# Attention and a mixture of experts on one core: the later attention lays the left block's scores over masked columns and turns each tile with three transposes

## The chip, the cores and the metric

One core of a Trainium2 chip runs the whole program in one launch. Its engines are TensorE (PE, with its weight loads PEld), VectorE (DVE), ScalarE (ACT), GpSimd (POOL) and SyncE (SP, which here only issues DMAs). The metric is the device time of one execution in microseconds (us); the median of three is compared.

## The reference, cut to what matters

```python
scores = q @ k.T / sqrt(D)                       # B,H,S,D = 4,8,768,64
rel = pos[:, None] - pos[None, :]
keep = (pos[None, :] < n_global) | ((rel >= 0) & (rel < n_local))    # 8 and 96
scores += -slope[h] * dist                       # dist = rel, or n_local for a far global key
a = softmax(where(keep, scores, -1e9)); x = a @ v
out = sum_e p[:, e] * (relu(x @ w1[e]) @ w2[e])  # 3072 rows, 512 -> 1024 -> 512, 4 experts
```

A row of queries sees at most 96 keys back, and the first 8 keys. So a tile of 128 queries needs its own block of 128 keys, the last 96 keys of the block on its left, and the global keys (32 columns are kept for them).

## The kernel before, in words

There are three stages. The first is the attention of batch 0 alone (0 to about 60 us). The second runs the experts of batches 0 and 1 and, woven into them, the attention of batches 1, 3 and 2 (`attention_chain`, about 100 to 646 us). The third is the experts of batches 2 and 3 (to the end). The change is in the second stage alone, the "later attention".

The later attention goes over 3 batches x 4 pairs of heads x 6 query tiles: 72 tiles, of which 12 are the first of their sequence (t = 0, with no left block) and 60 have one. It is a pipeline that moves by one `flow()` at a time, twelve flows to a pair. Each flow does, for four different tiles:

- `scores`: four fp32r matmuls (two heads, high and low parts) into one PSUM tile `ps`, per head 256 columns: 96 of the left block, 32 global, 128 of the own block. For t = 0 only the 128 of the own block are used.
- `softmax` of the tile whose scores are newest: per head one VectorE instruction that subtracts the bias `nbias`, writes `pb` and gives the row's extremum `nmax`, and one ScalarE exponential; then, of the tile before, the reciprocal of the row sums and one ScalarE multiplication per head (`pb <- pb, zsum`).
- `turn` of the tile before that: one PE transpose for each 128 columns of `pb` (four, or two at t = 0) into one PSUM bank `pt`, and one ScalarE copy to `pT`.
- `weigh`, once per pair of heads, when all six tiles are turned: per tile and head, `pT`'s own part times `v`, plus its left-and-global part times `vg`, into two `pt` banks.

`vg` holds, per tile, the 96 rows of `v` left of it and the 32 global rows. `windows` makes it with one SBUF-to-SBUF DMA on SP and one GpSimd copy, once per pair. Pools of this stage: `pb` 2 buffers, `pT` 6, `ps` 2, `pt` 2, `vg` 1, `v` 1.

In the same stage GpSimd makes sums and low parts of the experts' weights (`sums`, `w1s`, `w2s`, `raw`), fed by DMAs of raw weights; they are made for a unit two units ahead. An order is kept in program order only while `Ordered.on` is set or an engine is held; from step 14 of batch 0 on, where the attention's generator has run its first piece, a planner orders each engine's queue by priority and its own costs, and the queues then run in that order on the chip. How often a flow is emitted is paced by the matmul groups done (`paced`, `count`, `span`). All engines' calls go through the helper at L43, so nearly every row of the profile has that line; tiles tell them apart.

Of the kernel before, what the change touches and what calls it, by code (L numbers as in the profile page):

```python
# [186 lines left out]
def attn_moe_kernel(ctx: ExitStack, tc, q, k, v, n_global, n_local, domain_probs, w1, w2, out):  # L187
# [40 lines left out]

    nbias = fast.tile([P, H, 3 * P], BF16, name="nbias")

    def biases(sp):
# [152 lines left out]
    def windows(A, vt):  # L384
# [4 lines left out]
        return vg  # L389

    def scores(A, t, got):
# [13 lines left out]
        return [both[:, j] for j in range(2)]  # L405

# [13 lines left out]
    def softmax(A, new, old):  # L420
# [4 lines left out]
        if new:  # L425
            t, pr, ps = new["t"], new["pr"], new["ps"]
            cols = slice(0, P) if t == 0 else slice(0, 2 * P)
            bcol = slice(2 * P, 3 * P) if t == 0 else slice(0, 2 * P)
            new["pcol"] = pcol = slice(P, 2 * P) if t == 0 else slice(0, 2 * P)
            nmax = A.small.tile([P, 2], F32, name="nmax")  # L430
            new["zsum"] = A.small.tile([P, 2], F32, name="zsum")
            new["pb"] = A.pb.tile([P, 2, 2 * P], F32, name="pb")
        for j in range(2):
# [17 lines left out]
        if old:  # L451
            for j in range(2):
                p = pb[:, j, old["pcol"]]
                if A.early:
# [3 lines left out]
                else:  # L458
                    ac.activation(p, p, AF.Copy, scale=zsum[:, j : j + 1])

    def turn(A, tile_):
# [9 lines left out]
        tile_["pT"] = pT  # L471

    def weigh(A, three, x, b):

        px = A.px.tile([P, 512], F32, name=A.pxname)
        for i, tile_ in enumerate(three):
            t, pr, pT = tile_["t"], tile_["pr"], tile_["pT"]
            vt, vg = tile_["v"]["v"], tile_["v"]["vg"]
            for w in range(1 if t == 0 else 0, 2):
                for j in range(2):  # L480
                    vv = vt[:, j, t] if w == 1 else vg[:, j, t - 1]
                    te.matmul(
                        px[j * D : (j + 1) * D, i * P : (i + 1) * P],
                        vv,
                        pT[:, w, j, :],
                        start=(w == 1 if t == 0 else w == 0),
                        stop=(w == 1),
                    )
# [81 lines left out]
    def attention_chain(bs, A):  # L570
# [5 lines left out]
        def flow(new=None):  # L576

            one, two, three, four = tiles
            if new:
                new["ps"] = scores(A, new["t"], gots[new["m"]])  # L580
            if four:
# [6 lines left out]
            if three:  # L588
                turn(A, three)
            softmax(A, one, two)  # L590
# [7 lines left out]

        fetch_heads(0, "qkv")
        yield  # L600
        for m, (b, pr) in enumerate(order):
# [9 lines left out]
            for t in range(NQT):  # L611
                if t in (1, 2, 3):
                    if t == 1:
                        prepare_k(A, nat["k"], 1, got)
                    elif t == 2:
                        fetch_heads(m + 1, "qk")
                    else:
                        nat["vg"] = windows(A, nat["v"])
                    flow()
# [833 lines left out]
```

## Time and profile before

| | |
|---|---|
| median of three runs | 1162.91 us (1162.72 to 1163.08) |
| span of the profiled execution | 1162.9 us |
| PE / PEld busy | 1140.5 / 1062.6 us (98% / 91%) |
| DVE / ACT / POOL busy | 853.2 / 618.2 / 606.6 us (73% / 53% / 52%) |
| chain that ended last | PE 87%, DVE 5%, ACT 3%, POOL 2%, DMA 1% |

A matmul's record is longer than the time by which it moves the next one on, since matmuls are pipelined: the cost of a matmul is read as the distance from its start to the next start, not as its duration. An instruction's row names what it writes and reads (`pt<-ident,pb` is a transpose of `pb` into `pt`). The profiled execution and the median agree, so a sum made against the span holds for the median.

### The profile page before, as it was taken

The page shows a single profiled execution, that of the slowest core. Times are in us where ns is not written, and L with a number is a line of the kernel's source. Part 1 is how long each engine was busy: PE and PEld are TensorE (multiplying, and loading weights), DVE is VectorE, ACT ScalarE, POOL GpSimd, SP SyncE. Part 2 cuts the span into 40 slices and gives each one's busy share as a digit, 9 for nine tenths or more (in the row PEclk, how much of TensorE's full clock was granted, in tenths as well). Part 3 has the DMA queues.
Part 4 walks back from the last instruction along what each step waited for, and adds up shares of the span by engine and source line. Part 5 has one row for each costly group of instructions (what it writes and reads, how often), then busy time and mean ns, then how long its engine had stood idle before and what let it go on. Part 6 is the DMA issues. An engine that isn't in the chain of part 4 may idle for free.

```text
span 1162.9 us, 21146 instructions
## 1 busy us (share of the span) xinstructions
PE 1140.5 (98%) x7474; PEld 1062.6 (91%) x7474; DVE 853.2 (73%) x1944; ACT 618.2 (53%) x1597; POOL 606.6 (52%) x592
## 2 busy tenths in 40 slices
PE   7899999999999999999999999999999999999997
PEld 5678898989888989899998899999999999999997
DVE  7977776767767777776776777777777777777776
ACT  6854767777653665655565334444445444444443
POOL 5676645554343314222222327777778855555554
PEclk9999999999999999999999999999999999999999
DMA  9558798778775889978868668888887687777764
GB/s 185 149 172 290 268 294 258 269 253 255 247 261 206 282 269 286 282 234 279 257 196 288 207 215 304 306 302 300 284 314 281 240 303 239 249 247 247 245 232 131
DMA packets 181744, 294.32 MB, mean 253 GB/s; under 512 B 86400, under 2 KB 137088, under 8 KB 169344
## 3 DMA queue, kind: packets, MB, share of 16 engines
q1 hardware_dynamic: 177600, 286.61, 75.0%
q10 hardware_dynamic: 4032, 6.30, 1.5%
q8 instruction: 61, 1.00, 0.4%
q14 instruction: 51, 0.42, 0.1%
HBM read 207.93 MB, written 70.78 MB: 240 GB/s over the span
## 4 chain that ended last, share of the span: by engine, by line
PE 87%; DVE 5%; ACT 3%; POOL 2%; DMA 1%; issue 1%; DVEq 0%; ACTq 0%; POOLq 0%
PE pm L43 36%; PE pf L43 19%; PE X L43 11%; PE Y L43 9%; PE pt L43 7%; PE ps L43 4%; ACT pb L43 1%; DVE pb L43 1%; POOL w1s L43 1%; PE px L43 1%; DVE acc L43 1%; DVE xB L43 1%; DMA x_last<-piece 0%; DVE hA L43 0%; DVE pm L43 0%
## 5 line engine op out<-in xcount | busy, mean ns | idle before, releaser
L43 PE MATMUL pm<-w2s,h 128*128 128x512 f32 x1152 | 282.8, 395 | 3.6 <-DVE h L43 2.6
L43 PEld LDWEIGHTS pm<-w2s,h 128*128 128x128 f32 x1152 | 210.7, 188 | 46.5 <-DVE h L43 4.5
L43 ACT ACTIVATE hf<-pf 128x384 f32<-128x384 f32 x128 | 62.8, 491 | 248.3 <-DVE pf L43 247.1
L43 POOL TENSOR_TENSOR hS<-sf,hS 128x384 fp32r<-128x384 f32 x126 | 134.3, 1084 | 113.0 <-ACT hS L43 112.2
L43 DVE SCALAR_TENSOR_TENSOR acc<-pm,prob,acc 128x512 f32<-128x512 f32 x180 | 132.4, 748 | 54.5 <-PE pm L43 53.6
L43 POOL TENSOR_TENSOR sums<-raw 128x256 f32<-128x256 f32 x54 | 39.2, 745 | 211.8 <-DMA raw<-in_moe_w_dram 133.4
L43 PE MATMUL pm<-xT,w1s 128*128 128x384 f32 x744 | 147.9, 341 | 0.0
L43 PE MATMUL pf<-xT,w1s 128*128 128x384 f32 x768 | 146.5, 335 | 0.9 <-ACT hf L43 0.7
L43 PEld LDWEIGHTS pf<-xT,w1s 128*128 128x128 f32 x768 | 131.4, 188 | 1.7 <-ACT hf L43 1.2
L43 PEld LDWEIGHTS pm<-xT,w1s 128*128 128x128 f32 x744 | 128.0, 188 | 0.7 <-issue 0.7
L43 ACT ACTIVATE pb<-pb,nmax 128x256 f32<-128x256 f32 (+1 forms) x192 | 94.2, 498 | 58.1 <-DVE nmax L43 54.2
L43 DVE TENSOR_TENSOR hA<-hf,hA 128x384 fp32r<-128x384 f32 x94 | 84.6, 925 | 50.6 <-ACT hA L43 49.1
L43 PE MATMUL pm<-xB,w1s 128*128 128x384 f32 x574 | 116.8, 344 | 0.1
L43 PE MATMUL pf<-xB,w1s 128*128 128x384 f32 x576 | 110.7, 335 | 0.2 <-ACT hf L43 0.2
L43 PEld LDWEIGHTS pm<-xB,w1s 128*128 128x128 f32 x574 | 99.9, 188 | 5.5 <-issue 1.4
L43 ACT ACTIVATE h<-pm 128x384 fp32r<-128x384 f32 x128 | 62.0, 490 | 74.4 <-DVE pm L43 73.3
L43 PEld LDWEIGHTS pf<-xB,w1s 128*128 128x128 f32 x576 | 98.7, 188 | 0.6 <-ACT hf L43 0.4
L43 POOL TENSOR_TENSOR sf<-hf 128x384 f32<-128x384 f32 x63 | 70.3, 1116 | 43.6 <-ACT hf L43 43.6
L43 DVE CUSTOM_DVE_ANT_0 pb<-ps,nbias 128x256 f32<-128x256 f32 (+1 forms) x192 | 72.3, 395 | 5.8 <-PE ps L43 4.8
L43 DVE SCALAR_TENSOR_TENSOR h<-pm,h 128x384 fp32r<-128x384 f32 x128 | 69.5, 550 | 8.4 <-ACT h L43 6.8
L43 PE MATMUL Y<-w2b,hS 128*128 128x256 f32 x576 | 74.0, 282 | 0.0
L43 PE MATMUL X<-w2b,hS 128*128 128x256 f32 x576 | 73.9, 282 | 0.0
(159 smaller groups left out, 2183.5 us busy)
## 6 DMA issues: line engine op xcount, KB each, us to landing
w1s<-kept SPq DMA_DIRECT2D x47, 1792.0 KB, 8.2
w2b<-kept SPq DMA_DIRECT2D x224, 256.0 KB, 4.3
kept<-w1s SPq DMA_DIRECT2D x16, 1792.0 KB, 7.3
raw<-in_moe_w_dram SPq DMA_DIRECT2D x43, 512.0 KB, 4.7
kept<-w2s SPq DMA_DIRECT2D x16, 1024.0 KB, 6.9
w2s<-kept SPq DMA_DIRECT2D x16, 1024.0 KB, 5.5
qd<-qd SPq DMA_DIRECT2D x48, 192.0 KB, 3.2
v<-in_v_dram SPq DMA_DIRECT2D x16, 384.0 KB, 4.1
```

Source lines behind the costliest of these rows:

```text
L43: ins = fn(*args, **kwargs)
```

## The change

For tiles with a left block (t > 0) of the later attention:

- After the scores, a VectorE predicated copy lays the 96 left columns over columns 32 to 127 of the own block wherever that column's key lies after the query (mask `newer`, made once). The two never overlap: own key c is seen by query r if c <= r, the left key in column c if c > r.
- The bias is folded in the same way, once, by a minimum over `nbias`. Softmax then works on 160 columns (32 global, 128 folded) in place of 256.
- The normalised values go to a new tile `pn` of 320 columns by three ScalarE copies: own of head 0, global of head 0 (32 columns), global and own of head 1.
- `turn_folded` makes three transposes: own of head 0, own of head 1, and one that has both heads' globals in its first 64 columns. ScalarE copies own (256 columns) and, twice, 32 rows of globals. Two GpSimd affine selects (rows 32 to 63 and 64 to 127) copy the left part out of the folded block into `pT[:, 0]`, zero elsewhere.
- `pT[:, 1]` still has both parts, so `weigh` multiplies it by `v` of the own tile and `pT[:, 0]` by a difference: `differences` replaces `windows`, one GpSimd subtraction of neighbouring `v` tiles and one copy of the global rows; the DMA goes.

```diff
+    newer = fast.tile([P, NPREV], BF16, name="newer")
+    def differences(A, vt):
+        vd = A.vg.tile([P, 2, NQT - 1, D], F32, name="vg")
+        po.tensor_sub(vd, vt[:, :, : NQT - 1], vt[:, :, 1:])
+        po.tensor_copy(vd[:NGLOB], vt[:NGLOB, :, 0:1, :].to_broadcast([NGLOB, 2, NQT - 1, D]))
...
+            if t and not A.early:
+                own = new["both"][:, :, P + NGLOB :]
+                ve.copy_predicated(own, newer.bitcast(mybir.dt.uint16)[:, None, :].to_broadcast([P, 2, NPREV]), new["both"][:, :, :NPREV])
...
-            new["pb"] = A.pb.tile([P, 2, 2 * P], F32, name="pb")
+            new["pb"] = A.pb.tile([P, 2, width], F32, name="pb")
...
-                    ac.activation(p, p, AF.Copy, scale=zsum[:, j : j + 1])
+            old["pn"] = pn = A.pb.tile([P, 2 * PL], F32, name="pn")
+            glob = () if old["t"] == 0 else ((0, pn[:, P:PL], pb[:, 0, :NGLOB]),)
+            own = pn[:, PL:] if glob else pn[:, PL + NGLOB :]
+            for j, dst, src in ((0, pn[:, :P], pb[:, 0, NGLOB:]), *glob, (1, own, pb[:, 1, old["pcol"]])):
+                ac.activation(dst, src, AF.Copy, scale=zsum[:, j : j + 1])
+    def turn_folded(A, tile_):
+        t, pn = tile_["t"], tile_["pn"]
+        pt = A.pt.tile([P, 4, P], F32, name="pt")
+        pT = tile_["pT"] = A.pT.tile([P, 2, 2, P], F32, name="pT")
+        for place, at in enumerate((0, PL + NGLOB, P)[: 3 if t else 2]):
+            te.transpose(pt[:, place, :], pn[:, at : at + P], ident)
+        ac.copy(pT[:, 1], pt[:, :2])
+        if t:
+            for j in range(2):
+                ac.copy(pT[:NGLOB, 0, j], pt[j * NGLOB : (j + 1) * NGLOB, 2])
+            for rows in (slice(P // 4, P // 2), slice(P // 2, P)):
+                po.affine_select(
+                    pT[rows, 0], pT[rows, 1], pattern=[[0, 2], [-1, P]], compare_op=ALU.is_gt, fill=0.0,
+                    base=rows.start, channel_multiplier=1,
+                )
...
         fetch_heads(0, "qkv")
+        po.iota(
+            newer, pattern=[[1, NPREV]], base=NGLOB, channel_multiplier=-1, allow_small_or_imprecise_dtypes=True
+        )
+        po.tensor_scalar(newer, newer, 0.0, 1.0, op0=ALU.is_gt, op1=ALU.mult)
+        own = nbias[:, :, P + NGLOB : 2 * P]
+        ve.tensor_tensor(own, own, nbias[:, :, :NPREV], op=ALU.min)
...
-                        nat["vg"] = windows(A, nat["v"])
+                        nat["vg"] = differences(A, nat["v"])
```

## Rows read from the trace of the kernel before

**Rows 1.** The page: busy time by engine; PE's busy tenths in 40 slices

```profile
PE 1140.5 (98%) x7474; PEld 1062.6 (91%) x7474; DVE 853.2 (73%) x1944; ACT 618.2 (53%) x1597; POOL 606.6 (52%) x592
...
PE   7899999999999999999999999999999999999997
```

**Rows 2.** Busy us (instructions) by stretch, then granted clock, DMA share, GB/s

```profile
100.00:650.00 550.00, 546.37 (x3387) 495.68 (x3385) 401.04 (x950) 342.07 (x919) 210.80 (x207) 1.00 0.79 256
720.00:760.00 40.00, 40.00 (x287) 40.00 (x285) 30.04 (x52) 17.17 (x42) 32.33 (x32) 1.00 0.90 314
```

**Rows 3.** Groups of PE, 100:650: count | busy us, mean ns | idle before

```profile
L43 PE MATMUL pt<-ident,pb 128*128 128x128 f32 x264 | 41.3, 273 | 0.9 <-ACT pb L43 0.8
```

**Rows 4.** Timeline of PE, two turns: start us, merged length, count

```profile
145.31 0.49 PE L43 MATMUL pt<-ident,pb 128*128 128x128 f32 x3
145.55 0.60 PE L43 MATMUL pm<-xT,w1s 128*128 128x384 f32 x2
...
464.20 0.60 PE L43 MATMUL pt<-ident,pb 128*128 128x128 f32 x4
464.55 1.29 PE L43 MATMUL pm<-xT,w1s 128*128 128x384 f32 x6
```

**Rows 5.** Groups of DVE, 100:650, shapes apart

```profile
L43 DVE CUSTOM_DVE_ANT_0 pb<-ps,nbias 128x256 f32<-128x256 f32 x120 | 47.1, 418 | 4.0 <-PE ps L43 3.0
...
L43 DVE CUSTOM_DVE_ANT_0 pb<-ps,nbias 128x128 f32<-128x128 f32 x24 | 6.3, 281 | 0.0
```

**Rows 6.** Groups of ACT, 100:650, shapes apart

```profile
L43 ACT ACTIVATE pb<-pb,zsum 128x256 f32<-128x256 f32 x120 | 54.7, 503 | 10.3 <-DVE zsum L43 9.9
...
L43 ACT COPY pT<-pt 128x512 f32<-128x512 f32 x60 | 35.1, 585 | 8.7 <-PE pt L43 7.9
...
L43 ACT ACTIVATE pb<-pb,zsum 128x128 f32<-128x128 f32 x24 | 8.5, 396 | 1.9 <-DVE zsum L43 1.9
...
L43 ACT COPY pT<-pt 128x256 f32<-128x256 f32 x12 | 4.4, 364 | 0.2
```

**Rows 7.** Groups of POOL, whole span, shapes apart

```profile
L43 POOL TENSOR_TENSOR sums<-raw 128x256 f32<-128x256 f32 x54 | 39.2, 745 | 211.8 <-DMA raw<-in_moe_w_dram 133.4 <-DMA kept<-sums 54.2 <-DMA qd<-qd 24.0
...
L43 POOL COPY vg<-v 32x768 f32<-32x768 f32 x16 | 13.1, 821 | 33.6 <-DMA v<-in_v_dram 20.7 <-PE pm L43 12.2
...
L43 POOL TENSOR_TENSOR xB<-x,xB 128x768 fp32r<-128x768 f32 x6 | 11.0, 1845 | 0.0
...
masks.py:199 POOL TENSOR_SCALAR_AFFINE_SELECT ident<-ident 128x128 f32<-128x128 f32 x1 | 0.3, 292 | 0.1
```

**Rows 8.** Waits of PE, 100:650: total us, times, longest

```profile
PE pt L43 <- ACT pb L43: 0.8, 2, 0.4
```

**Rows 9.** DMA issues, 100:650: KB each, median us to landing

```profile
vg<-v SPq DMA_DIRECT2D x12, 288.0 KB, 6.5
```

**Rows 10.** Timeline of ACT: copies of a pair's last turned tile

```profile
146.03 0.59 ACT L43 COPY pT<-pt 128x512 f32<-128x512 f32 x1
...
397.52 0.59 ACT L43 COPY pT<-pt 128x512 f32<-128x512 f32 x1
...
479.56 0.59 ACT L43 COPY pT<-pt 128x512 f32<-128x512 f32 x1
```

**Rows 11.** Timeline of PE: `weigh` of a pair's last tile begins

```profile
149.62 0.39 PE L43 MATMUL pt<-pT,vg 128*64 128x128 f32 x4
...
402.40 0.39 PE L43 MATMUL pt<-pT,vg 128*64 128x128 f32 x4
...
483.48 0.39 PE L43 MATMUL pt<-pT,vg 128*64 128x128 f32 x4
```

**Rows 12.** Timeline of POOL near these: [idle before <- what ended it]

```profile
150.88 1.42 POOL L43 TENSOR_TENSOR sums<-raw 128x256 f32<-128x256 f32 x2 [7.67 <-DMA raw<-in_moe_w_dram]
...
153.08 0.74 POOL L43 TENSOR_TENSOR sums<-raw,sums 128x256 f32<-128x256 f32 x1
...
403.73 1.43 POOL L43 TENSOR_TENSOR sums<-raw 128x256 f32<-128x256 f32 x2 [12.42 <-DMA kept<-sums]
...
407.86 2.40 POOL L43 TENSOR_TENSOR sums<-sums,raw 128x1024 fp32r<-128x1024 f32 x1
...
480.98 2.38 POOL L43 TENSOR_TENSOR sums<-sums,raw 128x1024 fp32r<-128x1024 f32 x1
```

More of the change, by code (lines that the diff above doesn't have):

```diff
@@ L389, in windows @@
         return vg
+    def differences(A, vt):
+        vd = A.vg.tile([P, 2, NQT - 1, D], F32, name="vg")
+        po.tensor_sub(vd, vt[:, :, : NQT - 1], vt[:, :, 1:])
+        po.tensor_copy(vd[:NGLOB], vt[:NGLOB, :, 0:1, :].to_broadcast([NGLOB, 2, NQT - 1, D]))
+        return vd
     def scores(A, t, got):
@@ L404, in scores @@
                 )
-        return [both[:, j] for j in range(2)]
+        return both
     def scores_early(A, t0, got):
@@ L426, in softmax @@
             t, pr, ps = new["t"], new["pr"], new["ps"]
-            cols = slice(0, P) if t == 0 else slice(0, 2 * P)
-            bcol = slice(2 * P, 3 * P) if t == 0 else slice(0, 2 * P)
-            new["pcol"] = pcol = slice(P, 2 * P) if t == 0 else slice(0, 2 * P)
+            first = 0 if A.early else NPREV
+            cols = slice(0, P) if t == 0 else slice(first, 2 * P)
+            bcol = slice(2 * P, 3 * P) if t == 0 else slice(first, 2 * P)
+            width = 2 * P - first
+            new["pcol"] = pcol = slice(width - P, width) if t == 0 else slice(0, width)
+            if t and not A.early:
+                own = new["both"][:, :, P + NGLOB :]
+                ve.copy_predicated(own, newer.bitcast(mybir.dt.uint16)[:, None, :].to_broadcast([P, 2, NPREV]), new["both"][:, :, :NPREV])
             nmax = A.small.tile([P, 2], F32, name="nmax")
             new["zsum"] = A.small.tile([P, 2], F32, name="zsum")
-            new["pb"] = A.pb.tile([P, 2, 2 * P], F32, name="pb")
+            new["pb"] = A.pb.tile([P, 2, width], F32, name="pb")
         for j in range(2):
@@ L451, in softmax @@
         if old:
-            for j in range(2):
-                p = pb[:, j, old["pcol"]]
-                if A.early:
+            if A.early:
+                for j in range(2):
+                    p = pb[:, j, old["pcol"]]
                     ve.tensor_scalar(
@@ L457, in softmax @@
                     )
-                else:
-                    ac.activation(p, p, AF.Copy, scale=zsum[:, j : j + 1])
+                return
+            old["pn"] = pn = A.pb.tile([P, 2 * PL], F32, name="pn")
[3 more added lines that the diff above has]
+                ac.activation(dst, src, AF.Copy, scale=zsum[:, j : j + 1])
     def turn(A, tile_):
@@ L471, in turn @@
         tile_["pT"] = pT
+    def turn_folded(A, tile_):
[6 more added lines that the diff above has]
+        if t:
+            for j in range(2):
+                ac.copy(pT[:NGLOB, 0, j], pt[j * NGLOB : (j + 1) * NGLOB, 2])
[4 more added lines that the diff above has]
+                )
     def weigh(A, three, x, b):
@@ L478, in weigh @@
             vt, vg = tile_["v"]["v"], tile_["v"]["vg"]
-            for w in range(1 if t == 0 else 0, 2):
+            parts = (1,) if t == 0 else (0, 1)
+            for w in parts:
                 for j in range(2):
@@ L485, in weigh @@
                         pT[:, w, j, :],
-                        start=(w == 1 if t == 0 else w == 0),
+                        start=(w == parts[0]),
                         stop=(w == 1),
@@ L579, in flow @@
             if new:
-                new["ps"] = scores(A, new["t"], gots[new["m"]])
+                new["both"] = scores(A, new["t"], gots[new["m"]])
+                new["ps"] = [new["both"][:, j] for j in range(2)]
             if four:
@@ L588, in flow @@
             if three:
-                turn(A, three)
+                turn_folded(A, three)
             softmax(A, one, two)
```

## The prediction, made before the result was known

> **What bounds the kernel now.** I read the page's busy line first: PE is busy 98% of the span, and its slices stand at 9 from the second to the last but one [rows 1]. A busy PE is not yet a full PE, so the windows come next. In the stretch of the later attention, 100 to 650 us, PE is busy 546.4 of 550 us at full granted clock, DVE 401, ACT 342, POOL 211 [rows 2]. After it PE stays the bound: at 720 to 760 its matmuls and its weight loads are both busy 40.0 of 40 us [rows 2]. So time taken from PE's queue in the middle should come off the end, as nothing behind it has slack to swallow it, provided that the other engines still feed PE in time. Of those, DVE is the fullest, at 73% of the stretch. What PE waits for is small: the attention's own chain held it up for 0.8 us (two transposes that waited for the normalised values) [rows 8]. A change here can win mainly by giving PE less to do, and can lose by a new wait.
>
> **What is removed from PE.** The 264 transposes of the stretch are 12 pairs of heads x (5 tiles x 4 + 1 tile x 2) [rows 3]. The change takes one from each of 60 tiles. Their price is not the 273 ns of a record: where four stand together, the next matmul starts 0.35 us after the first (464.20 to 464.55); where three stand together, 0.24 us (145.31 to 145.55) [rows 4]. The fourth is worth 0.11 us; the plain average of four would be 0.09. So 60 x 0.11 = 6.6 us (5.3 by the average), all on the path. Scores (four matmuls of 256 columns) and weighing keep their counts and shapes: those matmuls cost the same.
>
> The Trainium skill, "TensorE: Matmul & The Clock Gate", Part 4: PE-mode transpose, gives about 275 ns for a 128x128 transpose inside a kernel, of which most is access latency. The records here agree as durations (273 ns), but their starts lie 0.11 us apart; by the page's figure as a cost the gain would be an estimated 16.5 us, by the starts 6.6.
>
> **DVE.** The bias instruction takes 418 ns at 256 columns and 281 at 128 [rows 5], so 144 ns and 1.07 ns a column: 315 ns at 160, two per tile, 0.21 us less. The predicated copy has no row. It moves 2 x 96 = 192 columns within PSUM; priced like the bias instruction, 0.35 us. Its bounds are 0.28 (the 128-column row) and 0.70 (if it took two passes). I take 0.35, as its shape lies between the two rows. Net +0.14 us per tile, 60 tiles: +8.6 us (4 to 30). DVE goes from 401 to 410 of 550 us (at most 431). The copy waits for the scores just as the bias instruction did, so no engine is newly waited for. Behind it on DVE stand the adds that free the experts' PSUM tiles, for which PE waits; 0.14 us fits into DVE's idle quarter.
>
> **ACT.** By the normalising rows, 503 ns at 256 and 396 at 128 columns [rows 6], an activation of 160 takes about 423 and one of 32 about 316. Two exponentials are shorter by 0.16 us together (priced by these rows, as their shapes are the same). Normalising becomes 396 + 423 + 316 in place of 2 x 503: +0.13. The copy to `pT` falls from 585 (512 columns) to 364 (256) [rows 6], but two copies of 128 columns come, about 254 each: +0.29. Net +0.26 us per tile, 15 us in all, on an engine busy 342 of 550. What hides it is that idle third; without it, 15 us would be the price. `pb` is now freed by ACT's normalising and not by PE's transposes, so the next tile's bias instruction waits for less. I give that nothing, at best the 0.8 us of [rows 8].
>
> **POOL.** An affine select of 128 columns took 292 ns in the setup [rows 7]. The new ones have 256 columns: 0.29 (if size is free) to 0.58; I take 0.45, as every POOL row here grows with its columns. Two per tile: 0.9 us, 54 us in all (35 to 70). The subtraction of 640 columns, between the rows of 256 (745 ns) and 768 (1845 ns), takes 1.57 us, and the copy of globals 0.68 in place of 0.82 [rows 7]: +1.43 per pair, 17 us in all. POOL goes from 211 to about 282 of 550 us. As a sum that is harmless. Behind a select that waits for ACT's copy stand the sums and low parts of expert weights; they are made two units ahead, so a microsecond there costs nothing. The other direction is the open point: who stands before a select (below).
>
> **DMAs.** The 12 window copies (288 KB, 6.5 us to landing [rows 9]) leave SP's queue and the DMA engines, busy 79% of the stretch [rows 2]. PE waited for none of them. I give this nothing.
>
> **Setup.** The mask's two small POOL instructions and the minimum over 8 x 96 = 768 columns on DVE (0.97 us by the slope above) run while queues are still in program order. Bounds 0 and 1.6 us (both on the path, the two POOL ones at 0.3 each); I take 0.5.
>
> **The new wait.** `weigh` now needs POOL. The selects can start when ACT has copied the folded block, 0.36 us after its start. For three pairs that is 146.39, 397.88 and 479.92 [rows 10]; with 0.9 us for two selects they would be done at 147.3, 398.8 and 480.8. PE takes up the pair's last tile at 149.62, 402.40 and 483.48 [rows 11]. So 2.3 to 3.6 us are spare, if POOL is free. If not, every matmul behind `weigh` stands still, since PE's queue is in order. POOL's state then differs [rows 12]: it waits for a DMA at its queue's head until 150.88 and until 403.73, and at 480 it is in the last step of a chain that ends at 483.36. Whether a select stands ahead of such a head is decided by the planner's guess of when the DMA lands. Bounds: 0, and 15 us if all three stand behind the whole chain (worked out below). I take 1.0 us, near the lower end: in 550 us the present queues, ordered by the same planner, kept PE waiting only 3.6 us in all [rows 2].
>
> **Sum.** -6.6 + 0.5 + 1.0 = -5.1 us. The profiled span, 1162.9 us, and the median of the runs, 1162.91, are the same, so 1162.9 - 5.1 = 1157.8 us. A measurement of this kernel can tell about 0.2%, 2.3 us, from no change: faster means below 1160.6, slower above 1165.2.
>
> **Rivals.**
>
> *Nothing is given back.* Every select is in time, the setup is hidden, the two waits for ACT go: -6.6 - 0.8 = 1155.5 us. For it: POOL is idle 62% of the stretch. Against: twelve times a pair's weighing has to meet POOL.
>
> *A transpose costs its duration.* 60 x 0.273 = 16.4 us, 1146.5 us. Against it stand the start distances in [rows 4], from which the whole sum is made. 2%.
>
> *DVE or ACT becomes the path.* If DVE's 8.6 us all lay on it, -6.6 + 8.6 = +2.0, 1164.9 us; half of it, 1160.6. For it: DVE feeds PE's PSUM tiles in small steps all through the stretch, and the predicated copy may cost twice my price. Against: a quarter of DVE stays idle. No measurable change in most of this case. The same band holds the case that a single pair meets a late DMA (next).
>
> *POOL's queue order, the slower side.* In a pair like that of 146 us the selects stand behind the chain that waits for its DMA: it starts at 150.88 and ends at 153.82, with the selects 154.8, and PE wanted them at 149.62: 5.2 us. In one like that of 397 us the chain ends at 410.26, selects 411.3, wanted 402.40: 8.9 us. In one like that of 480 us the chain ends at 483.36, selects 484.4, wanted 483.48: 0.9 us. Together 15.0: -6.6 + 0.5 + 15.0 = +8.9, 1171.8 us. It decides from the point where the blocked pairs cost over 8.4 us, thus from two such pairs (one of the dearer kind nearly does). For it: POOL did wait for a DMA at its head just then in two of the three pairs shown. Against: it was idle there because it had nothing else; a ready select may well be placed ahead.
>
> *The change doesn't do what it says.* Three transposes for four are plain in the code; I give this no chance of its own.
>
> **How the numbers follow.** Forecast, 1156.5 to 1160.5: 0.50. Nothing given back, 1154 to 1156.5: 0.13. Full duration: 0.02. DVE, ACT or one blocked pair, 1160.6 to 1165.2: 0.19. POOL's order, above 1165.2: 0.16. So faster 0.65, the same 0.19, slower 0.16. The range 1154.5 to 1167.0 leaves out about 0.04 below and 0.12 above.
>
> **What would show it.** In the stretch after the change: 204 transposes of `pn` in place of 264 of `pb`, three together moving the next matmul by 0.24 us; bias instructions near 0.32 us and predicated copies near 0.35; selects near 0.45 us; DVE near 410 of 550. The new wait shows as PE waiting for POOL's `pT` at `weigh`, twelve places; under 2 us in sum is my forecast, 5 us or more at one place is the slower rival. If PE's waits for DVE (`h`, `acc`) grow instead, it is the third rival. The stages after 650 us should keep their length and only start earlier; if they grow, the gain went there, which nothing here foresees.

## The result: 0.7% slower, with every instruction at its price

The changed kernel takes 1172.28 us (median of four, 1171.19 to 1173.74), the kernel before 1162.99: ratio 1.0072, 95% interval 1.0056 to 1.0088. The forecast was 1157.8, the range ended at 1167.0. The profiled execution took 1171.19 us, its span is 1169.1.

The page of the changed kernel, busy time by engine and the granted clock of PE in 40 slices (compare [rows 1]):

```profile
PE 1136.3 (97%) x7414; PEld 1056.1 (90%) x7414; DVE 858.1 (73%) x2005; ACT 624.5 (53%) x1777; POOL 673.3 (58%) x726
...
PEclk9999999999999999899999999999999999999999
```

PE has 60 instructions less and 4.2 us less work, and yet the span is 6.2 us longer. One slice of the clock stands at 8, the one at 468 to 497 us.

Groups of the changed kernel, 100 to 650 us, shapes apart (count | busy us, mean ns | idle before; compare [rows 3, 5 to 7]):

```profile
L43 DVE CUSTOM_DVE_ANT_0 pb<-ps,nbias 128x160 f32<-128x160 f32 x120 | 35.3, 320 | 1.4
L43 PE MATMUL pt<-ident,pn 128*128 128x128 f32 x204 | 34.1, 273 | 0.0
...
L43 POOL TENSOR_SCALAR_AFFINE_SELECT pT<-pT 32x256 f32<-32x256 f32 x60 | 24.7, 411 | 132.3 <-ACT pT L43 122.6 <-DMA raw<-in_moe_w_dram 7.5
...
L43 DVE COPY_PREDICATED ps<-newer,ps 128x192 f32<-128x192 uint16 x60 | 21.2, 353 | 2.4 <-PE ps L43 2.3
...
L43 POOL TENSOR_TENSOR vg<-v 128x640 f32<-128x640 f32 x11 | 17.3, 1569 | 25.9 <-DMA v<-in_v_dram 21.5 <-PE pm L43 4.4
```

No instruction here costs much more than forecast: the predicated copy 353 ns (0.35 us forecast), the bias 320 (315), the selects 411 (450), the subtraction 1.57 us (1.57). The loss is in waits. Waits of PE in the changed kernel, 84 to 660 us (total us, times, longest; compare [rows 8]):

```profile
PE pt L43 <- POOL pT L43: 3.7, 3, 2.6
PE pm L43 <- DVE h L43: 3.0, 4, 1.9
PE pt L43 <- ACT pT L43: 2.5, 3, 1.0
PE ps L43 <- DMA qd<-qd: 2.4, 1, 2.4
```

To place them, I took the 287 ScalarE instructions that read a finished group of the experts' first layer (`h<-pm`, `hf<-pf`, `p<-pm`), the same in both kernels, and subtracted the start in the trace of before from the start in the other. Below, this difference is called the lag. A fall is gain, a step up is a loss at that place. It counts from 93 us on: at 84 us some runs already lie up to 2.2 us off, most of them after some us with the granted clock at 0.50 near 50 us, in the stage before (nine of the seventeen traces).

| us in the trace of before | 84 | 93 | 265 | 467 | 498 | 545 | 568 | 643 | 663 | 1129 |
|---|---|---|---|---|---|---|---|---|---|---|
| lag of the changed kernel | -0.9 | +1.6 | -1.0 | -2.7 | +3.6 | +3.0 | +4.6 | +3.3 | +6.1 | +6.2 |

So the transposes do give their gain: the steady fall is 4.3 us from 93 to 467, in which 39 of the 60 tiles are turned, 0.11 us each. Four places take it back: +2.4 at the start, +6.3 at 480, +1.6 before 568 and +2.8 at 649. Behind 663 us the lag stays, so the later stages keep their length.

**At 84 to 94 us.** Timeline of the changed kernel: POOL, ACT, PE (start us, length, [idle before <- what ended it]):

```profile
87.12 1.57 POOL L43 TENSOR_TENSOR vg<-v 128x640 f32<-128x640 f32 x1
...
91.01 0.62 ACT L43 CAST w1s<-sums 128x512 fp32r<-128x512 f32 x1 [4.30 <-POOL sums L43]
...
94.05 2.11 PE L43 MATMUL pm<-w2s,h 128*128 128x512 f32 x8 [1.85 <-DVE h L43]
```

and of the kernel before, ACT:

```profile
89.42 0.62 ACT L43 CAST w1s<-sums 128x512 fp32r<-128x512 f32 x1 [1.89 <-POOL sums L43]
```

The first pair's differences stand on POOL ahead of the sums of weights, and so does the mask (two instructions from 83.79 to 84.65 us). ACT has the cast of those sums at the head of its queue and waits 4.30 us in place of 1.89; the `h` behind it comes late, and PE waits 1.85 us.

**At 480 us.** SP's timeline in the changed kernel, then PE's and POOL's:

```profile
472.43 0.33 SPq L43 DMA_DIRECT2D w2s<-kept  x1
472.86 5.40 SPq L43 DMA_DIRECT2D qd<-qd  x4
...
481.97 0.50 PE L43 MATMUL ps<-kd,qd 128*128 128x256 f32 x2 [2.40 <-DMA qd<-qd]
...
483.90 0.70 PE L43 MATMUL pt<-pT,vg 128*64 128x128 f32 x4 [0.24 <-POOL pT L43]
...
481.03 2.35 POOL L43 TENSOR_TENSOR sums<-sums,raw 128x1024 fp32r<-128x1024 f32 x1
483.45 0.40 POOL L43 TENSOR_SCALAR_AFFINE_SELECT pT<-pT 64x256 f32<-64x256 f32 x1
```

and SP's in the kernel before:

```profile
472.38 1.36 SPq L43 DMA_DIRECT2D qd<-qd  x2
475.35 0.34 SPq L43 DMA_DIRECT2D w2s<-kept  x1
```

Before, the first two transfers of `qd` (the second half of the turned queries, 192 KB each) went ahead of the 1 MB of `w2s`. Now `w2s` is at the head of SP's queue, waits there for PE until 472.43, and all four `qd` stand behind it. Meanwhile POOL is in a long sum of weights, and the last tile's second select ends at 483.85, so the weighing could not have gone on before that anyway. DMA issues (KB each, median us to landing) of the changed kernel from 472 to 474 us, the `w2s` and the first two `qd`,

```profile
w2s<-kept SPq DMA_DIRECT2D x1, 1024.0 KB, 9.1
qd<-qd SPq DMA_DIRECT2D x2, 192.0 KB, 9.0
```

and of the kernel before from 472 to 475 us, the first two `qd`:

```profile
qd<-qd SPq DMA_DIRECT2D x2, 192.0 KB, 4.5
```

The first `qd` is issued only 0.5 us later than before (472.86 for 472.38); it is the way to its landing that doubles. Landing by landing the trace shows why: `w2s` lands at 481.56 and the first `qd` 0.4 us behind it, at 481.93; the waiting matmul starts at 481.97. In all seventeen traces each of SP's transfers landed behind the one issued before it (543 neighbouring pairs in the changed kernel, 555 in the kernel before, no exception), so here a small transfer took as long as the 1 MB ahead of it.

Stretches of the changed kernel (busy us of PE, PEld, DVE, ACT, POOL; granted clock, DMA share, GB/s; the first compares with [rows 2]):

```profile
100.00:650.00 550.00, 540.29 (x3304) 487.12 (x3302) 402.97 (x1005) 347.49 (x1096) 274.57 (x337) 0.99 0.78 250
...
482.00:484.00 2.00, 1.76 (x14) 1.22 (x16) 0.00 (x0) 0.00 (x0) 1.78 (x2) 0.68 0.08 28
484.00:488.00 4.00, 4.00 (x15) 3.12 (x16) 0.51 (x4) 1.34 (x6) 0.00 (x0) 0.50 0.10 24
488.00:490.00 2.00, 2.00 (x9) 1.97 (x9) 0.63 (x2) 0.49 (x1) 0.00 (x0) 0.61 1.06 294
...
652.00:660.00 8.00, 8.00 (x40) 7.03 (x39) 5.39 (x9) 1.46 (x3) 0.00 (x0) 1.00 0.62 197
```

After the wait of 2.40 us the granted clock is at its lower level, 1.2 GHz, for some 7 us: 0.32 x 2 + 0.5 x 4 + 0.39 x 2 = 3.4 us more, an estimate that counts all work of the stretch as slowed in proportion. With the wait that is 5.8 of the 6.3 us.

**Before 568 us.** The same order again, SP and PE of the changed kernel:

```profile
559.40 0.33 SPq L43 DMA_DIRECT2D w2s<-kept  x1
559.83 5.66 SPq L43 DMA_DIRECT2D qd<-qd  x4
...
566.71 0.47 PE L43 MATMUL ps<-kd,qd 128*128 128x256 f32 x2 [0.57 <-DVE pm L43]
```

The profile puts this wait down to DVE, but the first `qd` lands at 566.58, again behind its `w2s` (566.01). In the kernel before two `qd` went ahead of that `w2s` too.

**At 649 us.** Timeline of the changed kernel, POOL and PE:

```profile
648.01 0.40 POOL L43 TENSOR_SCALAR_AFFINE_SELECT pT<-pT 32x256 f32<-32x256 f32 x1
648.50 2.34 POOL L43 TENSOR_TENSOR sums<-sums,raw 128x1024 fp32r<-128x1024 f32 x1
650.91 0.40 POOL L43 TENSOR_SCALAR_AFFINE_SELECT pT<-pT 64x256 f32<-64x256 f32 x1
...
651.36 0.44 PE L43 MATMUL pt<-pT,vg 128*64 128x128 f32 x4 [2.61 <-POOL pT L43]
```

The planner put one long sum of weights between the two selects of the pair's last tile, and the weighing waits 2.61 us for the second. Here the clock stayed at 1.00 (652 to 660 us above).

### The profile page after: what moved, and what is told of

It reads as the page before. It is cut to its first block, busy times and chain, and to the rows that moved or that the text cites. A ratio compares the mean times of both kernels' runs of the same rounds, so it can differ in the third digit from the quotient of the medians.

```text
span 1169.1 us, 21448 instructions
## 1 busy us (share of the span) xinstructions
PE 1136.3 (97%) x7414; PEld 1056.1 (90%) x7414; DVE 858.1 (73%) x2005; ACT 624.5 (53%) x1777; POOL 673.3 (58%) x726
## 4 chain that ended last, share of the span: by engine, by line
PE 69%; POOL 9%; DMA 9%; DVE 5%; ACT 5%; issue 2%; SPq 0%; POOLq 0%; ACTq 0%; DVEq 0%
PE pm L43 24%; PE pf L43 19%; PE X L43 11%; PE Y L43 9%; POOL sums L43 4%; PE pt L43 4%; DMA kept<-sums 4%; DMA raw<-in_moe_w_dram 3%; PE ps L43 2%; DVE pb L43 2%; ACT pb L43 1%; POOL w1s L43 1%; POOL w2s L43 1%; POOL pT L43 1%; ACT pn L43 1%
## 5 line engine op out<-in xcount | busy, mean ns | idle before, releaser
L43 POOL TENSOR_SCALAR_AFFINE_SELECT pT<-pT 32x256 f32<-32x256 f32 x120 | 49.0, 408 | 135.4 <-ACT pT L43 122.6
L43 ACT ACTIVATE pb<-pb,nmax 128x160 f32<-128x160 f32 (+2 forms) x192 | 84.0, 442 | 56.6 <-DVE nmax L43 52.4
L43 PE MATMUL X<-w2b,hA 128*128 128x256 f32 x576 | 73.8, 282 | 0.0
```

What stands on the lines that cost most here:

```text
L43: ins = fn(*args, **kwargs)
```

## The experiments

Ratios are to the kernel before, run on the same chip, with 95% intervals; the median of before there was 1164.4 to 1164.6 us.

### What the parts cost alone

**The changed kernel again**, unchanged.

> The changed kernel once more, as the measure for its variants on the same chip. Both theories: a span near 1169 us, with the four places in it at which the trace of after lost time: about 2.4 us at 84 to 94 us (ScalarE waits for GpSimd's weight sums), about 6.4 us from 479 us on (scores wait 2.4 us for the transfer of qd, then half clock to about 489), about 1.3 us near 566 to 570, and about 2.8 us near 648 (weighing waits for the last select). If the half clock is chance, it is missing here in some way and the span is 3 to 4 us shorter.

Measured 1172.95 us, 1.0073 (1.0056 to 1.009). The lag steps at the same places: +2.4 at the start, +4.9 between 467 and 498, +4.5 at 649. The last is larger than in the first trace because this time the clock fell there:

```profile
651.51 0.44 PE L43 MATMUL pt<-pT,vg 128*64 128x128 f32 x4 [2.69 <-POOL pT L43]
...
652.00:655.00 3.00, 3.00 (x13) 2.74 (x10) 1.37 (x2) 0.48 (x1) 0.00 (x0) 0.50 0.00 0
```

**Three transposes alone.** The kernel before with three transposes; the left part of the second head is left out of the turned block.

```diff
+                if not A.early and w0 == 0 and w == 0 and j == 1:
+                    continue
...
+        if A.early or w0:
+            ac.copy(pT[:, w0:], pt[:, w0:])
+        else:
+            ac.copy(pT[:, 1], pt[:, 1])
...
```

> The kernel before, with three transposes per tile in place of four and nothing else of the change; the fourth block of each tile is copied from the third's neighbour, so the left part of the second head is left out of the computation. Theory A (PE is the bound, a transpose is worth the distance of starts, 0.11 us): 60 x 0.11 = 6.6 us less than before, 1156.3 us, interval of the ratio about 0.993 to 0.996. Rival B (what PE gives up is refilled by waits for DVE and ACT, wherever it is taken): within 2.3 us of before.

Measured 1159.29 us, 0.9947 (0.9931 to 0.9964): 5.2 us under before. The lag falls from -0.9 at 93 us to -6.3 at 545, 5.4 us and on its way to the 6.6 forecast, but then steps to -2.3. SP and PE of this kernel at that step:

```profile
549.89 0.33 SPq L43 DMA_DIRECT2D w2s<-kept  x1
550.33 0.47 SPq L43 DMA_DIRECT2D qd<-qd  x1
...
559.19 0.50 PE L43 MATMUL ps<-kd,qd 128*128 128x256 f32 x2 [2.53 <-DMA qd<-qd]
```

So the gain is real, and a `qd` behind `w2s` costs 4 us in this execution even with no select and no predicated copy in the kernel.

**The same with the order of SP held.** As above, and the fetch of `w2s` in the second batch traced four steps later and held in its place on SP (still without the left part of the second head).

```diff
+            for _ in range(4):
+                yield 1
+            sy.held = True
             wts[(i, 2)] = fetch("w2s", (e, g, 2), [P, 2, 2, DM], lambda t: t)
+            sy.held = False
```

> The kernel before with three transposes in place of four per tile (the left part of the second head is left out of the turned block, as in the run with three transposes alone), and w2s held behind two of the qd issues on SyncE as in the run above. Theory A (a late qd behind 1 MB of w2s is a near tie in the order of SyncE which any shift of some us can lose, and not a matter of the selects): the wait of 2.5 us for qd at 556 us and the half clock after it go, the gain of 6.3 us at 545 us is kept to the end: 1157.5 to 1159 us, ratio 0.9935 to 0.995, under the 1159.3 us of the run without the hold. Rival B (the bunching of the transfers is the bound and comes back elsewhere): a wait for qd or a weight of over 1.5 us stands at another place, 1160 us or more.

Measured 1158.89 us, 0.9948 (0.9932 to 0.9965). In its profile PE waits for no `qd`, and the lag goes from +1.0 at 93 us to -5.5 at 663 without a step: -6.5, the forecast's -6.6. The median moved by only 0.4 us against the run above: there the profiled execution was the slowest of its four, so its stall need not be the price in every execution.

**The load on GpSimd alone.** The kernel before with two selects per tile on POOL whose output nothing reads.

```diff
+        if t and not A.early:
+            spare = A.st.tile([P, 2, P], BF16, name="spare")
+            for rows in (slice(P // 4, P // 2), slice(P // 2, P)):
+                po.affine_select(spare[rows], pT[rows, 1], ...
```

> The kernel before, with the two GpSimd selects per tile added on a spare tile that nothing reads: GpSimd's added work alone (about 49 us), without a new wait of PE. Theory A (GpSimd's work costs only where PE waits for its result): within 1.5 us of before. Rival B (more work on GpSimd delays the sums of weights, their transfers and so PE): 3 us or more above before.

Measured 1165.48 us, 1.0007 (0.9998 to 1.0017); the lag is +1.7 at 93 us and +1.8 at 663. Its stretch:

```profile
100.00:650.00 550.00, 546.63 (x3387) 495.65 (x3386) 399.98 (x947) 342.20 (x918) 261.56 (x329) 1.00 0.79 257
```

POOL carries 51 us more [rows 2] and PE loses nothing. The selects cost only where somebody waits for them.

### One cause taken away at a time

**The first pair's differences held in their place on POOL.**

```diff
+                        po.held = m == 0
                         nat["vg"] = differences(A, nat["v"])
+                        po.held = False
```

> The changed kernel, with the GpSimd work on the differences of v of the first pair of heads alone held behind what was traced before it on GpSimd. Theory A (the time is lost at single places, this is one): the wait of PE for h near 92 us (1.9 us) goes, span 2.4 us under after_again, the rest unchanged, the mask's 0.8 us on GpSimd may keep up to 0.8 of it. Rival B (GpSimd's and ScalarE's added work slows everything): no difference over 0.5 us.

Measured 1170.05 us, 1.0051 (1.0035 to 1.0068). The lag is -0.8 at 84 us and -0.6 at 93: the step of the start is 0.2 us and not 2.4, so the differences made nearly all of it, and the mask and the minimum are nearly free. Its other places stay. The stretch right after its wait of 2.85 us for `qd`:

```profile
481.00:483.00 2.00, 1.99 (x20) 1.33 (x18) 0.00 (x0) 0.00 (x0) 0.88 (x2) 1.00 0.06 23
```

In this execution the clock stayed, and the step at 480 is 3.8 us (-4.5 to -0.7) where it was 6.3.

**`qd` issued by ScalarE**, so that SP's order can't hold it.

```diff
-            sy.dma_start(f32(qd[oth, j]), f32(qd[own, j]))
+            ac.dma_start(f32(qd[oth, j]), f32(qd[own, j]))
```

> The changed kernel, with the transfers of qd issued from ScalarE's queue in place of SyncE's, so that they no longer stand behind a weight fetch of 1 MB there. Theory A (the late qd is a matter of the order on SyncE's queue, and the half clock follows from the stall): no wait of PE for qd near 479 us, full clock there, span 6 us under after_again, about 1163. Rival B (the transfer is late since the DMA engines are full, whatever the queue): the wait stays, within 1 us. Rival C: ScalarE waits at its head for VectorE's part of qd 24 times and PE's waits for ScalarE's h and pT grow by more than is won.

Measured 1174.13 us, 1.008 (1.0063 to 1.0097): no better, where theory A had about 1163. The wait for `qd` near 480 is gone, and PE's timeline of this kernel has in its place:

```profile
484.90 0.70 PE L43 MATMUL pt<-pT,vg 128*64 128x128 f32 x4 [3.99 <-POOL pT L43]
```

**`w2s` held behind two of the `qd`** (the diff of the held order above, on the changed kernel).

> The changed kernel with one thing moved on SyncE: in the feed-forward part of the second batch the 1 MB fetch of second-layer weights (w2s) is traced four steps later and held in its place in SyncE's order, so that two of the four issues of qd stand ahead of it, as in the kernel before, where the changed kernel has all four behind it. Theory A (the stall at 480 us is the queue's order: SyncE stands at the head for a buffer of w2s, and qd lands behind 1 MB): the wait of TensorE for qd near 480 us (2.40 us in the changed kernel's profile) and the half clock after it go, the curve of time against the kernel before no longer jumps by 6.3 us there, and the time is 4 to 6 us under the changed kernel: 1167 to 1169 us, ratio 1.002 to 1.004 against the kernel before. Rival B (the selects on GpSimd are the bound there and the wait for qd only hid them): a wait for pT of 2 to 4 us stands at 480 us in its place, followed by the half clock, and the time stays at 1172 to 1174 us.

Measured 1170.99 us, 1.0052 (1.0035 to 1.0068), between the two theories in time, but rival B by its waits: none for `qd`, one of 3.2 us for POOL at 485 with the clock at 0.50 behind it. Waits of PE:

```profile
PE pt L43 <- POOL pT L43: 7.7, 4, 3.2
```

The step at 480 is still 5.8 us (-1.8 to +4.0). Two ways of freeing `qd` uncover the same wait: near 480 us the changed kernel has two causes, one under the other, of 2.4 and 3 to 4 us. Whichever is mended alone, the other remains, with the lower clock behind it. The same holds at 568: here a wait of 1.41 us for POOL stands in the place of the one for `qd`, and the step is again 1.6 us. The 0.24 us for POOL that the profile of the changed kernel shows there is what the wait for `qd` left of it.

### Moving the weighing away from the selects

**Weighing one flow later**, selects first among POOL's ready work, the first differences held; nothing held on SP. The edit also fetches `v` one part of the pipeline later.

```diff
-            if four:
-                turned.append(four)
             if len(turned) == NQT:
...
                 turned.clear()
+            if four:
+                turned.append(four)
...
+            with tc.high_priority():
+                for rows in (slice(P // 4, P // 2), slice(P // 2, P)):
...
```

> The changed kernel without the hold on w2s, but with the weighing of four tiles one flow later, the selects first on GpSimd and the first pair's differences held in place. It leaves the four issues of qd behind w2s. Theory A (two causes of their own: selects and the queue): no wait of the weighing for GpSimd at 441, 569 and 649 us, the start costs 0.5 us and not 2.4, but the wait for qd near 477 us of 2 to 3 us and the half clock after it stay: 1163 to 1166 us, ratio 0.999 to 1.002, 4 to 6 us above the run with everything. Rival B (the late qd follows from a late weighing, since POOL and PE are late there): the wait for qd goes with the selects' waits, and the time is that of the run with everything within 1 us.

Measured 1174.09 us, 1.0076 (1.0059 to 1.0093). I missed it by 8 to 11 us. Waits of PE:

```profile
PE ps L43 <- DMA qd<-qd: 3.0, 1, 3.0
PE pt L43 <- ACT x L43: 2.9, 3, 2.0
```

No wait for POOL is left, as theory A said, and `qd` stays late. But the lag rises from +1.6 at 93 us to +8.2 at 265, before any of the places in question. PE waits at 156 us for a `pt` bank, which ScalarE's copy of the weighed half (`x`) frees, and ScalarE itself came late. Its timeline:

```profile
153.79 0.62 ACT L43 CAST w1s<-raw 128x512 fp32r<-128x512 f32 x1 [2.00 <-DMA qd<-qd]
...
155.69 0.48 ACT L43 COPY x<-pt 128x384 f32<-128x384 f32 x1
...
178.50 0.62 ACT L43 CAST w1s<-raw 128x512 fp32r<-128x512 f32 x1 [3.91 <-DMA raw<-in_moe_w_dram]
```

The raw weights that these casts read landed at 153.69 and 178.43; in the kernel before the two casts waited 0 and 0.2 us, with only the differences held 0 and 2.2. After the wait at 156 the clock was down as well (0.73 from 158 to 162 us). So this run lost its time to late weight transfers and to the clock, at new places; whether the later weighing or the moved fetch of `v` made them late isn't separated.

**Everything at once:** the same and `w2s` held.

> The changed kernel with all four causes met at once and nothing of the change taken out: w2s held behind two of the qd issues on SyncE, the first pair's differences held in their place on GpSimd, the two selects of a tile put first among what GpSimd can run, and the weighing of four tiles moved one flow later (the fetch of v one part later with it), so that a whole part of the pipeline lies between the selects and the matmuls that read them. Theory A (the change's own gain of some 6 us is there and four places outside the turning eat it): no stall of TensorE over 0.5 us at 93, 480, 569 and 649 us, and the curve against the kernel before falls to -4 to -6 us: 1157 to 1160 us, ratio 0.994 to 0.997. Rival B (many small waits of the longer chain over ScalarE and VectorE eat the gain wherever the four places are mended, as with the mask on VectorE): the curve stays between 0 and -2 us, 1162 to 1165 us, ratio 0.998 to 1.001. Rival C (another transfer comes late in the new order): a wait for a DMA of over 1.5 us at a new place, 1165 us or more.

Measured 1170.12 us, 1.005 (1.0033 to 1.0067). Theory A and rival B miss; rival C is nearest, but it is ScalarE and not PE that waits for the late transfer (4.15 us, for raw weights, at 175.6). The four places are gone from PE's waits, but those for `x` stay (2.9 us, four times, the longest 1.7), and the lag rises from +0.2 at 93 us to +5.5 at 265. One thing is clean in this pair of runs: from 467 to 498 us the lag goes from +7.2 to +10.8 without the hold and from +4.5 to +4.5 with it. Where no select is waited for, the order of SP alone is worth 3.6 us, with the clock at 1.00.

### Splitting on VectorE

**All tiles split by a mask on DVE** in place of the selects, first differences held.

```diff
+            ve.tensor_tensor(pT[:, 0], pt[:, :2], left[:, None, :].to_broadcast([P, 2, P]), op=ALU.mult)
...
-            for rows in (slice(P // 4, P // 2), slice(P // 2, P)):
-                po.affine_select(
...
```

> The changed kernel with the left part split off by one VectorE multiplication with a mask (256 columns from PSUM, about 0.42 us a tile, 25 us in all) in place of the two GpSimd selects, and the first differences held back as in vd_pinned. Theory A (weighing waits for selects that stand inside the chain of weight sums): no wait of PE for GpSimd's pT; 2.9 us less by the first differences and about 4 us less by the selects (2.7 near 648, 0.9 near 440, 0.5 near 570) than after_again, 1165 to 1167; the late qd near 479 and its half clock stay. Rival B (VectorE becomes the path with 25 us more): slower than vd_pinned, PE's waits for h and acc above 3 us.

Measured 1168.59 us, 1.0037 (1.0022 to 1.0051). No wait for POOL; `qd` is late at 481 (2.2 us; step +4.8). And the lag falls by 2.2 us only (+0.8 at 93, -1.4 at 467), where it fell by 4.3 with the selects.

**The same with `qd` from ScalarE.**

> As mask_dve_pinned, with qd's transfers from ScalarE's queue. Theory A (the loss is four places: first differences, qd, half clock after it, selects): all of them are gone and the 6.6 us of the transposes show: 1157 to 1159 on a chip where before takes 1163, ratio 0.994 to 0.997. Rival B (a late transfer of qd takes its place again, or VectorE's work shows): ratio 1.000 or more.

Measured 1166.02 us, 1.0015 (1.0005 to 1.0025), a miss: no wait of PE over 0.75 us in the stretch, and the lag is +3.2 at 93 and +2.3 at 663, a fall of only 0.9. The waits that the profile names don't hold the rest: all of PE's idle time from 100 to 650 us is 4.3 us, before it was 3.6. By the distances from start to start, the transposes take 8.0 us less than before from 93 to 663 us, and the matmuls of the experts' first layer (`pm`, with `w1s`) 7.2 us more. The 60 multiplications of 424 ns are 25 us on DVE, between ScalarE's copies, but that they are what slows those matmuls isn't shown; the last run below gives a measure of it.

**Selects first among POOL's ready work**, first differences held, `qd` from ScalarE.

> The changed kernel with its GpSimd selects given first priority in the planner's order (the second select of a tile then stands ahead of the last, 2.3 us step of the chain of sums in five places), the first differences held back, and qd's transfers from ScalarE's queue. Theory A: the wait of weighing near 648 falls from 2.7 to about 0.3 us, and those that qd_scalar showed near 480 and 568 (4.0 and 2.3 us) fall by 2.3 each; what is left is a first select behind a chain that started late, up to 1.7 us. Span 8 to 10 us under qd_scalar's 1172.7, 1163 to 1165. Rival B: priorities do not change what the planner takes as ready, no change in these waits.

Measured 1162.99 us, 0.999 (0.9981 to 1.0), 0.9% better than with `qd` from ScalarE alone, for two edits together. But waits for POOL of 1.4 us at 481 and 2.1 us at 563 remain: a select that is ready first still waits for the sum that has begun.

### The split on VectorE for the last tile alone

Only a pair's last tile is short of time: the others are turned whole flows before the weighing. So the last one is split by the mask on DVE (12 multiplications), the four between it and the first keep their selects, and the first differences are held. (A pair has six tiles; where the expectations below and above speak of four, six is meant.)

```diff
+            if t == NQT - 1:
+                ve.tensor_tensor(pT[:, 0], pt[:, :2], left[:, None, :].to_broadcast([P, 2, P]), op=ALU.mult)
...
+        if t and t < NQT - 1:
             for rows in (slice(P // 4, P // 2), slice(P // 2, P)):
...
```

**With the order of SP left as the changed kernel has it:**

> The run above without the hold on w2s: all four issues of qd stand behind the 1 MB of w2s on SyncE, as in the changed kernel. Theory A (the order of the queue alone costs a stall and the half clock after it): TensorE waits 2 to 3 us for qd near 475 us and the time is 4 to 6 us over the run above, ratio 0.9985 to 1.002. Rival B (qd is late only where GpSimd holds the weighing back): no wait for qd over 0.5 us and the same time as the run above within 1.5 us.

Measured 1167.61 us, 1.0018 (1.0003 to 1.0032). Its wait and one stretch after it:

```profile
PE ps L43 <- DMA qd<-qd: 2.7, 1, 2.7
```

```profile
486.00:488.00 2.00, 2.00 (x16) 1.57 (x13) 0.00 (x0) 0.00 (x0) 0.00 (x0) 0.50 0.01 4
```

**With `w2s` held behind two `qd`:**

> The changed kernel with the first pair's differences held in place on GpSimd, w2s held behind two of the qd issues on SyncE, and the split of the last tile of four done by one multiplication with a mask on VectorE (some 424 ns, 16 to 20 of them) in place of its two selects on GpSimd; the first three tiles keep theirs. Theory A (only the last tile's select is waited for, and the order of qd is the other cause): no wait of the weighing for GpSimd, no wait for qd over 0.5 us, the curve against the kernel before falls by 4 to 6 us over the stretch: 1158 to 1160.5 us where the kernel before takes 1164, ratio 0.9945 to 0.997. Rival B (VectorE's place in the chain eats the gain even in one tile of four, or another cost of the change is not found): the curve stays within 2 us of flat, ratio 0.998 to 1.002.

Measured 1159.64 us, 0.9959 (0.9945 to 0.9973): faster than both kernels, 5.0 us under the kernel before; the changed one was at 1.0073. SP, and all waits of PE from 100 to 660 us:

```profile
471.04 1.28 SPq L43 DMA_DIRECT2D qd<-qd  x2
473.88 0.34 SPq L43 DMA_DIRECT2D w2s<-kept  x1
```

```profile
PE pt L43 <- ACT pT L43: 2.6, 3, 1.0
PE pm L43 <- DVE h L43: 1.6, 3, 0.8
PE pm L43 <- DVE acc L43: 0.7, 1, 0.7
```

The lag goes from +2.5 at 93 us to -3.4 at 663 without a step, -5.9. Between the two runs the source differs only in the place of one kind of fetch, and that is worth 8.0 us of the median (executions of 1158.2 to 1161.0 us with the hold, 1162.6 to 1170.0 without). In the traces 6.1 us of it arise at 480 and 1.7 before 568, where without the hold all four `qd` stand behind a `w2s` again. At 480 the first two `qd` are issued 4.3 us earlier (471.04 for 475.32) and, with no 1 MB ahead of them, take 7.8 us to land and not 9.4.

**With `qd` from ScalarE instead:**

> The run last_dve_pinned with the transfers of qd issued by ScalarE instead of SyncE, so that no fetch of weights stands ahead of them. Theory A: no wait for GpSimd and none for qd after 120 us (one of about 1 us near 109 us, as with the selects first), ratio 0.995 to 0.9975, within 1.5 us of the run with w2s held. Rival B (ScalarE's issues lengthen its chain and cost the turning): small waits for pn and pT on ScalarE through the stretch, ratio 0.998 to 1.001.

Measured 1163.02 us, 0.999 (0.9981 to 0.9999): 3.4 us over the run with the hold where 1.5 was expected, thus a miss; the ratio is in rival B's range, but its small waits for ScalarE don't show. No `qd` is late near 480 us, but the lag falls by 3.7 us only (+1.8 at 93, -1.9 at 663). Against the run that splits all tiles on VectorE, also with `qd` from ScalarE, this one differs in 48 multiplications less on DVE, with POOL's selects in their place: the lag falls by 3.7 us and not by 0.9, so those 48 cost 2.8 us net (the two ratios, each against the kernel before on its own chip, lie 0.25% apart, 2.9 us). A `qd` from ScalarE takes a median of 4.6 us over the stretch, from SP with the hold 3.8. The Trainium skill ("DMA: Bandwidth & Descriptors", "Issuing engines are not separate DMA queues") says that issuing from several engines saves only the issuing sequencer's time; over the stretch the 4.6 for 3.8 us agrees with that: the transfers became no faster. What the other queue did change is who stands ahead: the first `qd` near 480, issued at 471.75, landed at 477.60, before a transfer that SyncE had issued at 466.09 (478.31).

## Why the prediction was wrong, step by step

- **What bounds the kernel**: right. PE stayed the bound, and the lag of 663 us is the lag of the end.
- **What is removed from PE**, -6.6 us: right. The three transposes alone with the order held gave -6.5, in the changed kernel itself 4.3 us show up to 467 us, 0.11 a tile. The records stayed at 273 ns and the starts 0.11 us apart, so the figure of the Trainium skill ("TensorE: Matmul & The Clock Gate", Part 4), read as a cost, would have been wrong by 10 us.
- **DVE and ACT**: prices right (320 and 353 ns; 416 and 254 for the 423 and 254 forecast; DVE 403 of 550 us for 410), cover mostly there. One small thing was missed: three copies free a `pt` bank later than one, and PE waits three times for ACT's `pT`, 2.5 us, in place of the 0.8 for `pb`. And how little of DVE's idle quarter can be used shows in the mask for all tiles: 48 multiplications, 20 us more in the turning chain, cost 2.8 us.
- **POOL as a sum**: right. 274.6 us of 550 (282 forecast), and the same load without a reader cost nothing.
- **Setup**, +0.5: the term was mis-sized, 2.4 measured. Mask and minimum, which I priced, cost 0.2. The first pair's differences, which I had among POOL's harmless sums, cost the rest. The argument "they are made two units ahead, so a microsecond there costs nothing" fails at the start, where ACT already stands with the cast of these sums at its head.
- **The new wait**, +1.0: mis-sized. The profile shows 3.7 us in three places, and another 3 to 4 us lay under the wait for `qd` at 480. The range to 15 held it; I took the low end because present queues kept PE waiting for little. That was evidence on orders in which no such reader existed. The mechanism was nearly the rival's: the selects stood inside the chain of sums, but where PE waited the chain was running and not waiting for its DMA. At 480 and 649 it was one sum of 2.34 us between the two selects. The pairs of 146 and 397 us, which carried 14.1 of the rival's 15.0 us, did not wait for POOL at all.
- **DMAs**, "I give this nothing": this step failed. It counted the transfers that leave and gave nothing to the order of those that stay. SP's queue was planned anew, a 1 MB fetch came ahead of four small ones at 480 and before 568, they landed behind it, and with the last tile's select out of the way this alone is 8.0 us. Three transposes without any other part, with the window DMAs still there, bring the same stall at another pair. So the order is near a tie, and that the leaving DMAs tipped it isn't shown; which change tips it can't be read from the trace of before. That it can tip could have been asked: SP's rows of before show two `qd` 3 us ahead of the large fetch, and I read no row of that queue.
- **What a wait costs**: no term for it. I took a wait at its length. At 480 us the 2.4 us of wait were followed by a stretch at half clock that cost some 3.4 us more.
- **The slower rival** gave 1171.8 us and the kernel takes 1172.3, by luck, since the causes were mostly others: of the steps in the lag, 2.4 + 6.3 + 1.6 + 2.8, only the last one and what lay hidden at 480 and 568 are selects that came late. Its own ends of the selects (154.8, 411.3, 484.4) lie some 0.1 us too late for the 0.9 us that two selects are given: 14.6 us and not 15.0, thus 1171.4.
- **The base**: the span leaves out 1.8 us of each execution (an execution of before with the span of 1162.9 took 1164.66), so the profiled one was no median one. As both kernels have it, it hardly moves the difference.

What stays open: which part of the change tipped SP's order, and why the clock fell after some waits and not after others.

## What to carry to other kernels

When an edit touches the instruction streams of a kernel whose queues are planned, look for the in-order queues with little to spare, small transfers behind a large one above all (on SP here they landed behind it, without exception), and price their tipping, also where the edit only takes DMAs away. A helper engine with idle time is free as load and dear as a step: before putting work for the next matmul there, find what single long instruction can stand in front of it, and give only the parts with slack to it. When one mended wait brings nothing, look for a second one under it before giving up the theory.

## What the hardware showed that was not expected

A wait of PE can cost more than twice its length. After waits of 2.4 us (the changed kernel, 480 us) and 2.7 us (the last-tile split without the hold) the granted clock was 0.50, the lower level, for 4 us and more. The length of the wait doesn't decide it: after 2.85 us at 478 with the differences held and 3.0 us with the later weighing the clock stayed at 1.00, while it fell to 0.50 after 2.12 us at 563 with the selects first. Nor does the program: at 649 us one execution of the changed kernel kept 1.00 after a wait of 2.61 us, and another fell to 0.50 after 2.69. In the last-tile split without the hold five executions with a mean granted clock of 0.994 to 0.996 took 1167.6 to 1170.0 us, three with 0.998 or 0.999 took 1162.6 to 1165.3. What the engine did just before the wait differs between these places, though at 649 us the program is the same; no run here separates it.

The landings of SP's transfers came in the order of their issue at every one of 543 neighbouring pairs, so the time to landing of a small transfer (4.5 us for two `qd` before, 9.0 in the changed kernel) tells what stood ahead of it, and not what it would take alone.
